# Fixed order of the first 512 tokens: k times u ahead of the copy of y, low parts one unit later, the third block's scans behind them

## The chip, the cores and the metric

The kernel runs on one core of a Trainium2 chip. The metric is device time in microseconds (us); the kernel before takes 1140.89 us, the median of three runs (1139.58 to 1141.2). TensorE is called PE, VectorE DVE, ScalarE ACT, GpSimd POOL and the queue that issues most transfers SP, as in the profile.

## What is computed

A linear attention over 768 tokens for 2 batches of 8 heads of width 48, then a two-layer SiLU network, then eight experts with ReLU, weighted by a table P that is normalised eight times over rows and columns:

```python
for t in range(S):                      # attention, per head
    cur = (u * k[t]) outer v[t]
    y[t] = r[t] @ (state + cur)
    state = w[t][:, None] * state + k[t] outer v[t]
x = silu(y @ w_in) @ w_out              # 1536 tokens, 384 -> 2048 -> 384
P = exp(x @ w_gate - max); 8 times: P /= P.sum(1); P /= P.sum(0); P *= N / E
out = sum_e P[:, e] * (relu(x @ w1[e]) @ w2[e])
```

## The kernel before

**Tiling.** The 1536 tokens are six blocks of 256; a unit is one block of one pair of heads, so a block has four units and the whole attention 24. Units 0 to 7 (the first two blocks, 512 tokens) are written out by `front()`, whose instructions keep the order in which they are written on each engine. Everything else (units 8 to 23, the split of the weights, the two networks) is ordered by a scheduler, which may put its instructions between those of `front()`.

**A unit** goes through five groups. `n_scan` (L180): on DVE a backward scan (`zf`, L191) and `kz` (L193); on ACT `uk`, k times u (L186). `n_q` (L196): PE multiplies `uk` (L202) and transposes `kz` (L207), ACT copies `kt` (L210), `tot` (L211) and, from unit 4 on, the state into a bank (L214). `n_x` (L220): on DVE a reciprocal (L223), a forward scan (L224) and `x` (L226). `n_s` (L228): PE's L233 needs `x`, its L238 needs `kt` and the state's copy. `n_m` (L241): DVE takes the banks to SBUF with L247, L248 and the scan over states L250. `n_y` (L253): PE makes y (L262, L264), ACT copies it to `ys` (L272), SP sends `ys` into the tile `x1` (L277). In `front()` step i emits unit i up to `n_s`, then `n_m` and `n_y` of unit i-1.

**High and low parts.** The matmuls of the networks work on a value as a high part rounded to fp32r and the low part that is left. `split_x1` (L426) makes them for a third of a block of y (128 of 384 rows): ACT casts `x1h` (L433), DVE subtracts to get `x1l` (L434). A third can be split once the copies of two neighbouring units have landed.

**Weights.** They come in 16 pieces of 768 KB, loaded from POOL (L91) into three buffers. A piece is brought from 64 to 32 bits on DVE (L135, L137, L138 in `narrow`), cast on ACT (`whi`, L113) and subtracted on DVE (`wlo`, L114). Piece 0 serves the first two steps of the first layer (L545 to L547, nine matmuls of 512 columns a step), piece 1 the first two of the second (L564 to L566), and so on in turn. The buffer of load 2 is the tile of `aux`, in which units 0 to 7 keep `tot`: it is free once L250 of unit 7 is done. ACT turns a bank of the first layer into `g` (L551) and `gh` (L552), DVE makes `gl` (L553).

**After the first two blocks**, `attn_a` (L307) takes the scans of units 8 to 11; the scheduler places them, and before the change it puts several among the instructions of unit 7. Each engine runs its queue in order.

Of the kernel before, what the change touches and what calls it, by code (L numbers as in the profile page):

```python
# [5 lines left out]
F32 = mybir.dt.float32  # L6
F32R = mybir.dt.float32r
I32 = mybir.dt.int32
ACTF = mybir.ActivationFunctionType
# [4 lines left out]
NP = H // 2  # L14
# [3 lines left out]
CH = 64  # L18
BLK = 256
# [4 lines left out]
OFF_K = OFF_R + BLK  # L24
OFF_V = OFF_K + BLK
ATW = OFF_V + 4 * D
LN = 64 + D
NU = 4 * NB
N4 = 2 * NP
# [4 lines left out]
C_U = C_ID + 128  # L34
# [21 lines left out]
class Pipeline:  # L56
# [123 lines left out]
    def n_scan(self, i):  # L180
        nc = self.nc
        p = i % NP
        at = self.at.pop(i)
        w, r, k = at[0:LN, 0:WPAD], *(at[0:LN, o:o + BLK].rearrange("p (c t) -> p c t", c=4) for o in (OFF_R, OFF_K))
        uk = self.q_p.tile([LN, 4, CH], F32, tag="rk", name="uk")
        nc.scalar.activation(uk, k, ACTF.Copy, scale=self.cst[0:LN, C_U + p:C_U + p + 1])  # L186
        zf, ef = (self.sc_p.tile([LN, 4, CH + 2], F32, tag=n, name=n) for n in ("zf", "ef"))
        kz = self.sc_p.tile([LN, 4, CH], F32, tag="kz", name="kz")
        zff, d1f = (t.rearrange("p c t -> p (c t)") for t in (zf, self.d1[i % 2]))
        n = WPAD  # L190
        nc.vector.tensor_tensor_scan(zff[:, n - 1::-1], w[:, n - 1::-1], d1f[:, n - 1::-1], 0.0,  # L191
                                     op0=ALU.mult, op1=ALU.add)
        nc.vector.tensor_mul(kz, k, zf[:, :, 2:CH + 2])  # L193
        self.st[i] = dict(zf=zf, ef=ef, kz=kz, r=r, w=w, uk=uk)

    def n_q(self, i):  # L196
        nc = self.nc
# [80 lines left out]

    def front(self):

        for i in range(N4 + 1):
            if i < N4:
                self.n_scan(i)
                self.n_q(i)
                self.n_x(i)
                self.warm(K['wm'])
                self.n_s(i)
                if i + 4 < NU:
                    self.attn_load(i + 4)
            if i == N4:  # L290
                self.split_pieces(1)
            if i > 0:
                self.n_m(i - 1)
                if i - 1 in K['gate']:
                    self.gates[self.n_dma] = self.attn_x(i - 1)[0:1, 1, 0, 0:1]
                    self.dma_pieces(self.n_dma + 1)
                self.n_y(i - 1)
                if i + 5 < NS:
                    self.attn_load_v(i + 5)
            if i > 2 and (i - 3) % NP > 0:  # L300
                self.split_x1((i - 3) // NP, (i - 3) % NP - 1)
        self.split_pieces(2)
        for j in (N4 - 2, N4 - 1):
            self.split_x1(j // NP, j % NP - 1)


    def attn_a(self, i):  # L307
        if i < NS:
            self.n_scan(i)
            self.n_x(i)  # L310
            return
        nc = self.nc
        p = i % NP
        at = self.at.pop(i)
        w = at[0:LN, 0:WPAD]
        r = at[0:LN, OFF_R:OFF_K].rearrange("p (c t) -> p c t", c=4)
        k = at[0:LN, OFF_K:OFF_V].rearrange("p (c t) -> p c t", c=4)
        vu = at[:, OFF_V:ATW].rearrange("p (j h e) -> p j h e", j=2, h=2)
        d1 = self.d1[i % 2]
        zf = self.sc_p.tile([LN, 4, CH + 2], F32, tag="zf", name="zf")  # L320
        ef = self.sc_p.tile([LN, 4, CH + 2], F32, tag="ef", name="ef")
        kz = self.sc_p.tile([LN, 4, CH], F32, tag="kz", name="kz")
        zff = zf.rearrange("p c t -> p (c t)")
        eff = ef.rearrange("p c t -> p (c t)")
        d1f = d1.rearrange("p c t -> p (c t)")
        n = WPAD
        nc.vector.tensor_tensor_scan(zff[:, n - 1::-1], w[:, n - 1::-1], d1f[:, n - 1::-1], 0.0,
                                     op0=ALU.mult, op1=ALU.add)
        nc.gpsimd.tensor_mul(kz, k, zf[:, :, 2:CH + 2])
        nc.vector.reciprocal(d1[:, :, 0:1], zf[:, :, 1:2])  # L330
        nc.vector.tensor_tensor_scan(eff, w, d1f, 0.0, op0=ALU.mult, op1=ALU.add)
        x = self.attn_x(i)
        if i < NS + 2:
            nc.gpsimd.memset(x[96:128, 1], 0.0)
        nc.vector.tensor_mul(x[0:64, 0], r[0:64], ef[0:64, :, 0:CH])
        nc.gpsimd.tensor_mul(x[64:LN, 1], r[64:LN], ef[64:LN, :, 0:CH])
        u = self.cst[0:LN, C_U + p:C_U + p + 1]
        rk = self.q_p.tile([LN, BLK], F32, tag="rk", name="rk")
        nc.vector.tensor_mul(rk, at[0:LN, OFF_R:OFF_K], at[0:LN, OFF_K:OFF_V])
        qh = self.q1_p.tile([LN, BLK], F32R, tag="qh", name="qh")  # L340
        ql = self.q1_p.tile([LN, BLK], F32R, tag="ql", name="ql")
        nc.scalar.activation(qh, rk, ACTF.Copy, scale=u)
        nc.vector.scalar_tensor_tensor(ql, rk, u, qh.bitcast(F32), op0=ALU.mult, op1=ALU.subtract)
        self.st[i] = dict(zf=zf, kz=kz, vu=vu, qh=qh, ql=ql)
# [79 lines left out]
        self.x1[blk] = self.x1_p.tile([128, 3, BLK], F32, tag="x1", name="x1")  # L424

    def split_x1(self, blk, c):  # L426
        nc = self.nc
        x1 = self.x1[blk]
        tb, h = divmod(blk, 2)
        if h == 0 and c == 0:  # L430
            self.xs[tb] = tuple(self.xs_p.tile([128, 3, 2 * BLK], F32R, tag="xs", name=n) for n in ("x1h", "x1l"))
        hi, lo = (t[:, :, h * BLK:(h + 1) * BLK] for t in self.xs[tb])
        nc.scalar.copy(hi[:, c, :], x1[:, c, :])  # L433
        nc.vector.tensor_sub(lo[:, c, :], x1[:, c, :], hi[:, c, :].bitcast(F32))  # L434

    def warm(self, n):

# [278 lines left out]
    def run(self):  # L716
        tc, nc = self.tc, self.nc
        with ExitStack() as ctx:
# [6 lines left out]
            self.wg = cst_p.tile([128, 3, E], F32, name="wg")  # L725
            self.ones = cst_p.tile([128, 128], F32, name="ones")
            self.P = cst_p.tile([128, 13, E + 1], F32, name="P")
            self.xs, self.x1, self.x2, self.x2s, self.h, self.acc, self.at, self.st = ({} for _ in range(8))
            gen = self.general
            if gen:  # L730
                nc.sync.dma_start(out=self.cst, in_=self.ins["cst"])
# [83 lines left out]
            for i in range(len(steps) + 2):  # L815
                if i < len(steps):
                    s = steps[i]
                    if s[0] == "m":
                        _, tb, o, n, f = s
# [19 lines left out]
                    else:  # L839
                        _, e, tb, f = s  # L840
# [3 lines left out]
                if i >= 2:  # L844
                    s = steps[i - 2]
                    if s[0] == "m":
                        _, tb, o, n, f = s
# [5 lines left out]
                    else:  # L853
                        _, e, tb, f = s
# [82 lines left out]
```

## Time and profile before

| What | Value |
|---|---|
| median of three runs | 1140.89 us |
| the profiled execution, its own time | 1140.3 us |
| span of the profiled execution | 1138.5 us |
| PE busy | 1111.7 us, 98% of the span |
| DVE busy | 477.4 us, 42% |
| ACT busy | 322.7 us, 28% |
| POOL busy | 152.9 us, 13% |

The shares are means over the program. In the first 80 us PE has gaps and its granted clock changes between its two levels, 1.2 and 2.4 GHz (0.5 and 1.0 in the rows below); later it does not. "Idle" in a row is the time just before an instruction, with what ended it; a start minus the start ahead of it is how long an engine was held by one instruction, a little less than its own duration.

### The profile page before, as it was taken

Reading aid. Unit: us, or ns where it says so; the run is one execution under the profiler, and the core shown is the slowest. Engines: PE = TensorE matmul, PEld = TensorE weight load, DVE = VectorE, ACT = ScalarE, POOL = GpSimd, SP = SyncE. Lnnn points to the kernel's source line nnn. Section 1 sums busy time; section 2 is a strip of 40 time slices with the busy share of each in tenths; the row PEclk is TensorE's granted clock in tenths of the full one; section 3 lists DMA queues with packets and bytes.
Section 4 is the critical chain, followed back from the end, with each engine's and each line's share of the span. In section 5 each row is a group of like instructions: output and inputs, shape, how many; then the busy total and the mean of one; then the engine's idle time right before and its main releaser. Section 6 shows DMA issues by size and latency. Waiting matters only on the chain.

```text
span 1138.5 us, 17570 instructions
## 1 busy us (share of the span) xinstructions
PE 1111.7 (98%) x7376; PEld 1003.5 (88%) x7376; DVE 477.4 (42%) x873; ACT 322.7 (28%) x615; POOL 152.9 (13%) x129
## 2 busy tenths in 40 slices
PE   7789999999999999999999999999999999999997
PEld 7668889999989999999999999889999989999996
DVE  6699767784443311222212422652364231222221
ACT  3344444444642242122113112321332231111110
POOL 1011111110640030013004001200220130000000
PEclk8779999999999999999999999999999999999999
DMA  6265412110330011002001300440252020000000
GB/s 197 82 230 175 137 49 70 57 36 9 112 112 1 1 59 53 1 21 91 1 1 56 111 1 4 163 139 29 83 167 84 1 84 1 1 1 1 28 29 31
DMA packets 26920, 71.26 MB, mean 63 GB/s; under 512 B 4128, under 2 KB 11280, under 8 KB 26832
## 3 DMA queue, kind: packets, MB, share of 16 engines
q1 hardware_dynamic: 24528, 57.46, 16.2%
q0 software_dynamic: 2304, 12.58, 3.5%
q8 instruction: 60, 0.98, 0.4%
q14 instruction: 28, 0.23, 0.1%
HBM read 65.31 MB, written 2.36 MB: 59 GB/s over the span
## 4 chain that ended last, share of the span: by engine, by line
PE 94%; DVE 2%; DMA 1%; ACT 1%; issue 0%; SPq 0%; DVEq 0%; ACTq 0%
PE bank L656 12%; PE bank L658 12%; PE bank L640 12%; PE bank L641 12%; PE bank L657 12%; PE bank L639 12%; PE bank L564 3%; PE bank L566 3%; PE bank L565 3%; PE bank L545 3%; PE bank L547 3%; PE bank L546 3%; PE bank L419 1%; PE bank L356 1%; DMA lv<-in_vn_dram 1%; PE bank L233 0%
## 5 line engine op out<-in xcount | busy, mean ns | idle before, releaser
L645 DVE SCALAR_TENSOR_TENSOR hl<-bank,hh 128x512 fp32r<-128x512 f32 x192 | 132.3, 690 | 434.4 <-ACT hh L644 434.0
L656 PE MATMUL bank<-whi,hh 128*128 128x384 f32 x768 | 258.9, 337 | 0.7 <-ACT hh L644 0.7
L657 PE MATMUL bank<-wlo,hh 128*128 128x384 f32 x768 | 258.2, 336 | 0.0
L658 PE MATMUL bank<-whi,hl 128*128 128x384 f32 x768 | 254.2, 337 | 0.0
L644 ACT ACTIVATE hh<-bank 128x512 fp32r<-128x512 f32 x192 | 114.6, 598 | 489.0 <-PE bank L641 478.4
L641 PE MATMUL bank<-x2h,wlo 128*128 128x512 f32 x576 | 227.9, 396 | 0.0
L640 PE MATMUL bank<-x2l,whi 128*128 128x512 f32 x576 | 227.5, 395 | 0.0
L639 PE MATMUL bank<-x2h,whi 128*128 128x512 f32 x576 | 224.5, 390 | 0.0
L114 POOL TENSOR_TENSOR wlo<-raw,whi 128x768 fp32r<-128x768 f32 x64 | 118.2, 1858 | 564.7 <-ACT whi L113 547.1
L656 PEld LDWEIGHTS bank<-whi,hh 128*128 128x128 f32 x768 | 144.3, 188 | 9.4 <-ACT hh L644 1.1
L657 PEld LDWEIGHTS bank<-wlo,hh 128*128 128x128 f32 x768 | 144.2, 188 | 8.0 <-issue 0.2
L658 PEld LDWEIGHTS bank<-whi,hl 128*128 128x128 f32 x768 | 143.9, 188 | 2.4
L641 PEld LDWEIGHTS bank<-x2h,wlo 128*128 128x128 f32 x576 | 108.0, 188 | 22.4
L639 PEld LDWEIGHTS bank<-x2h,whi 128*128 128x128 f32 x576 | 108.2, 188 | 17.2 <-issue 0.2
L640 PEld LDWEIGHTS bank<-x2l,whi 128*128 128x128 f32 x576 | 108.0, 188 | 17.2
L113 ACT CAST whi<-raw 128x768 fp32r<-128x768 f32 x64 | 53.3, 836 | 94.2 <-PE bank L640 40.9
L545 PE MATMUL bank<-x1h,whi 128*128 128x256 f32 (+1 forms) x240 | 74.2, 311 | 3.8 <-ACT g L551 2.8
L564 PE MATMUL bank<-gh,whi 128*128 128x256 f32 (+1 forms) x240 | 74.8, 317 | 0.0
L669 DVE SCALAR_TENSOR_TENSOR acc<-bank,P,acc 128x384 f32<-128x384 f32 x84 | 48.0, 611 | 63.7 <-PE bank L658 63.7
L546 PE MATMUL bank<-x1l,whi 128*128 128x256 f32 (+1 forms) x240 | 73.8, 308 | 0.0
L547 PE MATMUL bank<-x1h,wlo 128*128 128x256 f32 (+1 forms) x240 | 73.6, 308 | 0.0
L566 PE MATMUL bank<-gh,wlo 128*128 128x256 f32 (+1 forms) x240 | 73.2, 306 | 0.0
(156 smaller groups left out, 1131.8 us busy)
## 6 DMA issues: line engine op xcount, KB each, us to landing
raw<-in_moe_w_dram SPq DMA_DIRECT2D x64, 384.0 KB, 3.8
raw<-in_moe_w_in_dram POOLq DMA_DIRECT2D x8, 768.0 KB, 4.9
raw<-in_moe_w_out_dram POOLq DMA_DIRECT2D x8, 768.0 KB, 4.7
wh<-in_moe_w_in_dram SPq DMA_DIRECT2D x8, 768.0 KB, 4.3
wh<-in_moe_w_out_dram SPq DMA_DIRECT2D x8, 768.0 KB, 4.2
at<-in_att_dram SPq DMA_DIRECT2D x12, 484.0 KB, 3.5
at<-in_att_dram SPq DMA_DIRECT2D x11, 339.5 KB, 4.4
wt<-in_w_dram SPq DMA_DIRECT2D x3, 768.0 KB, 4.3
```

The lines of the kernel that those rows point to most:

```text
L114: (nc.vector if i < N64 else nc.gpsimd).tensor_sub(lo, raw, hi.bitcast(F32))
L545: nc.tensor.matmul(ps, lhsT=wh, rhs=xh[:, d, :], start=(d == 0), stop=False)
L546: nc.tensor.matmul(ps, lhsT=wh, rhs=xl[:, d, :], start=False, stop=False)
L564: nc.tensor.matmul(ps, lhsT=wdh, rhs=gh, start=first, stop=False)
L639: nc.tensor.matmul(ps, lhsT=wh, rhs=xh[:, d, :], start=(d == 0), stop=False)
L640: nc.tensor.matmul(ps, lhsT=wh, rhs=xl[:, d, :], start=False, stop=False)
L641: nc.tensor.matmul(ps, lhsT=wl, rhs=xh[:, d, :], start=False, stop=(d == 2))
L644: nc.scalar.activation(hh, ps, ACTF.Relu)
L645: nc.vector.scalar_tensor_tensor(hl, ps, 0.0, hh.bitcast(F32), op0=ALU.max, op1=ALU.subtract)
L656: nc.tensor.matmul(ps, lhsT=hh[:, sl], rhs=wh, start=st, stop=False)
L657: nc.tensor.matmul(ps, lhsT=hh[:, sl], rhs=wl, start=False, stop=False)
L658: nc.tensor.matmul(ps, lhsT=hl[:, sl], rhs=wh, start=False, stop=sp)
```

## The change

`uk` becomes a function of its own, `n_uk`. `front()` emits it for unit i+1 right behind `n_q(i)`, so ahead of the copy of y of unit i-1. `split_x1` is cut in two: the cast stays where it was, the subtraction is emitted in the next step, behind `n_x` and ahead of `n_m`. Behind unit 7 comes piece 0 of the weights, then the subtractions that are left, then piece 1. The DVE instructions of `n_scan` and `n_x` of units 8 to 11 are given an edge to the last of these subtractions: they are queued behind it on DVE. Their `uk` on ACT has no such edge.

```diff
 def n_scan(self, i):
-    uk = self.q_p.tile([LN, 4, CH], F32, tag="rk", name="uk")
-    nc.scalar.activation(uk, k, ACTF.Copy, scale=self.cst[0:LN, C_U + p:C_U + p + 1])
...
+def n_uk(self, i):
+    uk = self.uk[i] = self.q_p.tile([LN, 4, CH], F32, tag="rk", name="uk")
+    self.nc.scalar.activation(uk, self.at[i][0:LN, OFF_K:OFF_V]..., ACTF.Copy, scale=...)
...
 def front(self):
+    lag = []
+    self.n_uk(0)
     for i in range(N4 + 1):
         if i < N4:
             self.n_scan(i)
             self.n_q(i)
+            if i + 1 < N4:
+                self.n_uk(i + 1)
             self.n_x(i)
             self.warm(K['wm'])
             self.n_s(i)
...
-        if i == N4:
-            self.split_pieces(1)
+        while lag:
+            self.split_x1_low(*lag.pop())
         if i > 0:
             self.n_m(i - 1)
...
         if i > 2 and (i - 3) % NP > 0:
-            self.split_x1((i - 3) // NP, (i - 3) % NP - 1)
+            lag.append(((i - 3) // NP, (i - 3) % NP - 1))
+            self.split_x1_high(*lag[-1])
+    self.split_pieces(1)
+    self.split_x1_low(*lag.pop())
+    for j in (N4 - 2, N4 - 1):
+        self.split_x1_high(j // NP, j % NP - 1)
+        self.front_end = self.split_x1_low(j // NP, j % NP - 1)
     self.split_pieces(2)
-    for j in (N4 - 2, N4 - 1):
-        self.split_x1(j // NP, j % NP - 1)

 def attn_a(self, i):
     if i < NS:
-        self.n_scan(i)
-        self.n_x(i)
+        self.n_uk(i)
+        with self.tc.issue_after(self.front_end):
+            self.n_scan(i)
+            self.n_x(i)
         return
```

The new lines shift the numbers: in the rows of the changed kernel L197 is `uk` (L186 before), L214, L215 and L218 are `kt`, `tot` and the state (L210, L211, L214), L276 is `ys` (L272), L448 and L453 are the cast and the subtraction (L433, L434), L189, L191, L227, L228 and L230 are the DVE steps of `n_scan` and `n_x`, L251, L252 and L254 those of `n_m`.

ACT's queue from unit 4 to unit 5, before and after:

```order
L214 COPY bank_67<-ss_131 112x48
L272 COPY ys<-bank_65 112x256
L433 CAST x1h<-x_301 128x256
L186 ACTIVATE uk<-at,cst 112x256
L210 COPY kt<-bank_64 128x192
```

```order
L218 COPY bank_67<-ss_131 112x48
L197 ACTIVATE uk<-at,cst 112x256
L276 COPY ys<-bank_65 112x256
L448 CAST x1h<-x_303 128x256
L214 COPY kt<-bank_64 128x192
```

`uk` of unit 5 has moved from behind the copy of y and the cast to ahead of both.

DVE's queue at the same place, from the last step of unit 3 (L250, L254) to the first step of `n_m` of unit 4:

```order
L250 SCALAR_TENSOR_TENSOR ss_134<-bank_64,aux 112x288
L434 TENSOR_TENSOR x1l<-x_301,x1h 128x256
L191 SCALAR_TENSOR_TENSOR zf<-at,d_127 112x264
L193 TENSOR_TENSOR kz<-at,zf 112x256
L223 RECIPROCAL d_127<-zf 112x4
L224 SCALAR_TENSOR_TENSOR ef<-at,d_127 112x264
L226 TENSOR_TENSOR x_129<-at,ef 112x256
L247 TENSOR_TENSOR x_128<-bank_66,cst 128x256
```

```order
L254 SCALAR_TENSOR_TENSOR ss_134<-bank_64,aux 112x288
L189 SCALAR_TENSOR_TENSOR zf<-at,d_127 112x264
L191 TENSOR_TENSOR kz<-at,zf 112x256
L227 RECIPROCAL d_127<-zf 112x4
L228 SCALAR_TENSOR_TENSOR ef<-at,d_127 112x264
L230 TENSOR_TENSOR x_129<-at,ef 112x256
L453 TENSOR_TENSOR x1l<-x_303,x1h 128x256
L251 TENSOR_TENSOR x_128<-bank_66,cst 128x256
```

The subtraction has moved behind the five steps of unit 5.

DVE's queue behind unit 7's last step (L250, L254), where `x_601` and `x_603` are the second block of y; in the rows of after the second `cv<-raw` is piece 2 (the tile that held `aux`), the third piece 1:

```order
L250 SCALAR_TENSOR_TENSOR ss_134<-bank_64,aux 112x288
L247 TENSOR_TENSOR x_128<-bank_66,cst 128x256
L193 TENSOR_TENSOR kz<-at,zf 112x256
L248 COPY_PREDICATED x_128<-cst,bank_66 128x256
L250 SCALAR_TENSOR_TENSOR ss_131<-bank_67,xx 112x288
L191 SCALAR_TENSOR_TENSOR zf<-at,d_127 112x264
L223 RECIPROCAL d_127<-zf 112x4
L224 SCALAR_TENSOR_TENSOR ef<-at,d_127 112x264
L434 TENSOR_TENSOR x1l<-x_601,x1h 128x256
L135 TENSOR_SCALAR cv<-raw 128x768 x2
```

```order
L254 SCALAR_TENSOR_TENSOR ss_134<-bank_64,aux 112x288
L135 TENSOR_SCALAR cv<-raw 128x768
L137 SCALAR_TENSOR_TENSOR cv<-raw,cv 128x768
L138 SCALAR_TENSOR_TENSOR cv<-raw,cv 128x768
L114 TENSOR_TENSOR wlo<-cv,whi 128x768
L453 TENSOR_TENSOR x1l<-x_603,x1h 128x256
L135 TENSOR_SCALAR cv<-raw 128x768
L453 TENSOR_TENSOR x1l<-x_603,x1h 128x256
L137 SCALAR_TENSOR_TENSOR cv<-raw,cv 128x768
L453 TENSOR_TENSOR x1l<-x_603,x1h 128x256
L135 TENSOR_SCALAR cv<-raw 128x768
L189 SCALAR_TENSOR_TENSOR zf<-at,d_126 112x264
```

Before, all of piece 0 and the scans of units 8 to 10 stood ahead of the first of these rows; now they stand behind it, the scans behind the last subtraction.

## Rows read from the trace of the kernel before

**Rows 1.** Windows: stretch, length; busy PE, PEld, DVE, ACT, POOL; clock; DMA, GB/s.

```profile
84.20:1130.00 1045.80, 1045.14 (x6344) 946.66 (x6343) 411.06 (x738) 291.94 (x543) 146.03 (x101) 1.00 0.17 54
```

**Rows 2.** Windows of DVE alone, units 3 to piece 8: stretch, length, busy.

```profile
16.00:98.50 82.50, 65.39 (x123) 0.83 0.51 160
```

**Rows 3.** DVE's waits in 9 to 98.6 us: total, times, longest.

```profile
DVE x1l L434 <- ACT x1h L433: 10.6, 3, 5.5
DVE xx L247 <- PE bank L233: 2.2, 2, 1.5
DVE gl L553 <- ACT gh L552: 1.6, 2, 1.3
DVE cv L135 <- DMA raw<-in_moe_w_in_dram: 0.7, 1, 0.7
DVE wlo L114 <- ACT whi L113: 0.6, 2, 0.4
```

**Rows 4.** DVE: start, duration, instruction, idle before; subtraction in unit 4, unit 7's end.

```profile
31.28 0.43 DVE L434 TENSOR_TENSOR x1l<-x,x1h 128x256 fp32r<-128x256 f32 x1 [5.49 <-ACT x1h L433]
...
58.06 0.75 DVE L250 TENSOR_TENSOR_SCAN ss<-bank,aux 112x288 f32<-112x288 f32 x1
```

**Rows 5.** ACT in order of time: copy of y, cast.

```profile
30.57 0.37 ACT L272 COPY ys<-bank 112x256 f32<-112x256 f32 x1 [1.84 <-PE bank L264]
30.84 0.41 ACT L433 CAST x1h<-x 128x256 fp32r<-128x256 f32 x1
```

**Rows 6.** PE's waits in 0 to 80 us for `uk`: total, times, longest.

```profile
PE bank L202 <- ACT uk L186: 6.5, 7, 1.2
```

**Rows 7.** Windows, columns of rows 1: one unit; three stretches.

```profile
31.25:35.65 4.40, 3.49 (x66) 3.08 (x67) 4.15 (x9) 1.30 (x4) 0.00 (x0) 0.75 0.28 60
...
20.00:33.40 13.40, 9.95 (x260) 8.94 (x256) 6.99 (x16) 4.28 (x12) 0.71 (x2) 1.00 0.59 176
36.70:40.20 3.50, 1.88 (x51) 1.60 (x47) 1.95 (x5) 1.08 (x3) 0.00 (x0) 0.98 0.10 29
40.20:43.50 3.30, 3.30 (x58) 2.99 (x55) 2.17 (x5) 0.90 (x3) 0.00 (x0) 0.51 0.48 134
```

**Rows 8.** POOL in order of time: the issue of load 2.

```profile
59.38 0.53 POOL L91 DMA_DIRECT2D raw<-in_moe_w_in_dram  x1 [37.71 <-DVE x L247]
```

**Rows 9.** The page's line of loads of 768 KB: median us to landing last.

```profile
raw<-in_moe_w_in_dram POOLq DMA_DIRECT2D x8, 768.0 KB, 4.9
```

**Rows 10.** Copies of y, issued 54.2 to 56.5; 61.2 to 62.4.

```profile
DMA to landing us min/median/max: 1.8/1.9/1.9
...
DMA to landing us min/median/max: 5.4/5.6/5.8
```

**Rows 11.** DVE in order of time, at piece 8 of the weights.

```profile
97.63 0.95 DVE L138 SCALAR_TENSOR_TENSOR cv<-raw,cv 128x768 int32<-128x768 int32 x1
98.50 0.55 DVE L135 TENSOR_SCALAR cv<-raw 128x768 int32<-128x768 int32 x1
```

**Rows 12.** ACT in order of time, up to unit 10's state copy.

```profile
102.16 0.60 ACT L551 ACTIVATE g<-bank 128x512 f32<-128x512 f32 x1 [1.01 <-PE bank L547]
102.65 0.31 ACT L210 COPY kt<-bank 128x192 f32<-128x192 f32 x1
102.85 0.85 ACT L113 CAST whi<-cv 128x768 fp32r<-128x768 f32 x1
103.58 0.63 ACT L552 CAST gh<-g 128x512 fp32r<-128x512 f32 x1
104.10 0.26 ACT L214 COPY bank<-ss 112x48 f32<-112x48 f32 x1
```

**Rows 13.** PE in order of time, up to the states of unit 10.

```profile
108.12 0.39 PE L564 MATMUL bank<-gh,whi 128*128 128x512 f32 x1
108.34 0.39 PE L565 MATMUL bank<-gl,whi 128*128 128x512 f32 x1
108.66 0.56 PE L238 MATMUL bank<-lv,kt 64*48 64x48 f32 x16
```

More of the change, by code (lines that the diff above doesn't have):

```diff
@@ L193, in n_scan @@
         nc.vector.tensor_mul(kz, k, zf[:, :, 2:CH + 2])
-        self.st[i] = dict(zf=zf, ef=ef, kz=kz, r=r, w=w, uk=uk)
+        self.st[i] = dict(zf=zf, ef=ef, kz=kz, r=r, w=w, uk=self.uk.pop(i))
+    def n_uk(self, i):
+        p = i % NP
+        uk = self.uk[i] = self.q_p.tile([LN, 4, CH], F32, tag="rk", name="uk")
+        self.nc.scalar.activation(uk, self.at[i][0:LN, OFF_K:OFF_V].rearrange("p (c t) -> p c t", c=4), ACTF.Copy,
+                                  scale=self.cst[0:LN, C_U + p:C_U + p + 1])
     def n_q(self, i):
@@ L426, in split_x1, with split_x1_high @@
     def split_x1(self, blk, c):
-        nc = self.nc
-        x1 = self.x1[blk]
+        self.split_x1_high(blk, c)
+        self.split_x1_low(blk, c)
+    def split_x1_high(self, blk, c):
         tb, h = divmod(blk, 2)
@@ L431, in split_x1, with split_x1_low @@
             self.xs[tb] = tuple(self.xs_p.tile([128, 3, 2 * BLK], F32R, tag="xs", name=n) for n in ("x1h", "x1l"))
-        hi, lo = (t[:, :, h * BLK:(h + 1) * BLK] for t in self.xs[tb])
-        nc.scalar.copy(hi[:, c, :], x1[:, c, :])
-        nc.vector.tensor_sub(lo[:, c, :], x1[:, c, :], hi[:, c, :].bitcast(F32))
+        self.nc.scalar.copy(self.xs[tb][0][:, c, h * BLK:(h + 1) * BLK], self.x1[blk][:, c, :])
+    def split_x1_low(self, blk, c):
+        tb, h = divmod(blk, 2)
+        hi, lo = (t[:, c, h * BLK:(h + 1) * BLK] for t in self.xs[tb])
+        return self.nc.vector.tensor_sub(lo, self.x1[blk][:, c, :], hi.bitcast(F32)).ins
     def warm(self, n):
@@ L727, in run @@
             self.P = cst_p.tile([128, 13, E + 1], F32, name="P")
-            self.xs, self.x1, self.x2, self.x2s, self.h, self.acc, self.at, self.st = ({} for _ in range(8))
+            self.xs, self.x1, self.x2, self.x2s, self.h, self.acc, self.at, self.st, self.uk = ({} for _ in range(9))
             gen = self.general
```

## The prediction

> **What bounds the kernel now.** I read the windows first, then the waits, then single instructions in order of time. From 84.2 us to 1130 PE is busy for 1045.14 of 1045.80 us at clock 1.00 [rows 1]. Behind 84.2 us nothing but PE's own work sets the end, and the change alters none of it. So the time can only move with how much of its work PE has done by the end of the front, and the end moves one for one with that. The reader should look for the engine that kept PE waiting before. From unit 3 to piece 8 of the weights DVE is busy 65.39 of 82.50 us [rows 2], idle 82.50 - 65.39 = 17.1. Its largest wait is for the cast `x1h`: 10.6 us in three waits, the longest 5.5 [rows 3]. There DVE is free at 31.28 - 5.49 = 25.8 and stands until the cast that follows `ys` is made [rows 4, 5], though five steps of the next unit's scans are ready behind it in its queue. PE meanwhile waits for `uk` seven times, 6.5 us together [rows 6], since `uk` stands on ACT behind the same copy and cast. The two waits feed each other: `ys` needs y, y comes late on a PE that waited for `uk`, and the subtraction waits for all of it. The narrowing of the weights comes behind this on DVE, so what DVE loses in the front arrives at the weights.
>
> **What the change removes.** `uk` ahead of `ys` needs only `at`, and a buffer that L202 of two units earlier has left; PE's waits of 6.5 / 7 = 0.93 each go. The subtraction one unit behind finds its cast made while DVE did the five steps of the next unit. Nearly the same DVE instructions stand ahead of L138 of piece 8 in both orders: the order of after has, net, three fewer steps of 128x256 of units 8 and 9 there. At 0.4 each, as L434 takes [rows 4], that is 1.1 us. So the sum is a ledger of DVE's idle time up to that step, which before hands on at 98.50 [rows 11].
>
> **What stays or comes anew**, term by term.
>
> *Subtractions.* The first still waits. Its cast follows `ys` of unit 3, which ended y at about 30.5 before; less three of the `uk` waits (2.7) this is 27.8, and with copy and cast (0.27 and 0.31 as queue steps [rows 5]) 28.5. DVE, free at 25.8 before, gains 1.9 on its waits for L233 (below), then does five steps, 2.5 of a unit's 4.15 [rows 7]: 26.4. Wait 2.1. The following units start from a PE that no longer waits, and I take nothing for them. The last needs unit 7's copies. Copies landed in 1.8 to 1.9 us while the queue was empty and in 5.4 to 5.8 around the time of the loads [rows 10]. In the order of after, loads 2 and 3 are under way there too. Counting from the end T of unit 7's L250: y and its copy 1.3, the last of the issues about 1.4 later, 5.6 to land, the cast 0.3, together 8.6. DVE gets to the last subtraction at T + 7.2. Wait 1.4; with 1.9 to land, none. Together 3.5, where 10.6 stood.
>
> *Banks of L233.* They waited 2.2 because PE came late with `uk`; I leave 0.6.
>
> *Loads.* Load 2 goes into `aux`, free with L250 of unit 7. That ended at 58.06 + 0.75 = 58.8, and POOL issued at 59.38 [rows 4, 8]: 0.6 later, and 4.9 to land [rows 9], so T + 5.4 or a little more. DVE has piece 0 (0.47 and three steps of 0.87), a wait for `whi` and one subtraction ahead of piece 2: T + 4.3. Wait 1.1. Before, seven steps of units 8 to 10 and all of piece 0 covered this. Load 6 waits in the same way for piece 3's buffer, 0.5 + 4.9 = 5.4 against 3.9 of DVE work queued: 1.5. Together 2.6, where 0.7 stood [rows 3].
>
> *Low parts of the weights.* `wlo` of piece 0 now follows its narrowing at once with the cast (0.73 as a queue step [rows 12]) between: 1.1, where 0.6 stood [rows 3].
>
> *Others.* Before: 17.1 - 10.6 - 2.2 - 0.7 - 0.6 = 3.0, of which 1.6 for `gh` [rows 3]. I take 1.6, bounds 1.0 and 3.0.
>
> *Unit 7 alone.* Scans of units 8 to 10 filled the gaps between its dependent steps; without them I estimate 0.5.
>
> Sum 3.5 + 0.6 + 2.6 + 1.1 + 1.6 + 0.5 = 9.9. So 17.1 - 9.9 = 7.2 less idle, with the 1.1 some 8.2, and piece 8's step hands on at 98.5 - 8.2 = 90.3.
>
> **From DVE to PE.** In the order of after the last wait of PE that I find stands in front of L242, the states of unit 10 (L238 before). It needs ACT's copy of the state, which is queued behind `whi` of piece 8 (0.73), `g` (0.49), `gh` (0.52), `kt` (0.20) and takes 0.2 [rows 12]; with 0.26 for the handings over, 2.4. PE begins it at 90.3 + 2.4 = 92.7, before at 108.66 [rows 13]: 16.0 earlier. But less of PE's work stands ahead of it: by the order 117 wide matmuls instead of 137, 20 at 108.34 - 108.12 = 0.22 to 0.23 each [rows 13], 4.55, and one unit's y less, 0.14. PE gains 16.0 - 4.7 = **11.3 us**. That this is more than DVE's 8.2 comes from slack: before, the split pieces lay some microseconds ahead of PE, and after they do not. Behind this, DVE needs less for a piece than PE, and PE stays supplied.
>
> The profiled execution took 1140.3, its span 1138.5; both move alike, to 1129.0. The median lies 0.6 higher: 1140.9 - 11.3 = **1129.6**.
>
> **Other moves.** SP: the load of unit 11's `at` stands behind unit 7's copies; its scans are now late on DVE, so nothing. POOL: loads 2, 3, 5, 4, 6 in this order, and unit 12's `kz` with a memset ahead of load 12, which waits about as long for the buffer of piece 9; nothing. ACT: the casts stand a `uk` later, 0.4, covered by the five steps of the next unit except at the first cast, where it is in the 2.1. The clock: for 13.4 us at 9.95 busy the granted clock stayed at 1.00 [rows 7], and after a thinner stretch, 1.88 of 3.5, it fell to 0.51 in the next [rows 7]. DVE's 4.15 us a unit now paces PE, whose 9.95 / 13.4 share rises, so I leave the front at full clock. The Trainium skill ("DMA: Bandwidth & Descriptors", section "Issuing engines are not separate DMA queues") says that transfers started by different engines run on the same 16 DMA engines and interleave. By it the copies of unit 7, issued from SP, share with POOL's loads of 768 KB; rows 10 agree. It speaks against moving subtractions close behind those copies: without it the 1.4 would be 0 and the time 1128.2.
>
> **Rivals.**
> *Faster still.* Copies land in 1.9 (1.4 less) and load 6 finds its buffer early enough (1.5 less, less 0.6 that PE can't take up): 13.6 in all, 1127.3. For it: the loads start earlier against the copies than before. Against it: 5.4 to 5.8 once measured [rows 10]. Chance 0.15.
> *The clock falls.* DVE alone serves units 5 to 7, and PE stands between units. If it goes to its lower level, as in 40.2 to 43.5 (0.51) after a stretch with PE busy for about half [rows 7], PE's part of a unit is as long as DVE's and y, `ys` and cast come later: some 2 us, 1131.5. The Trainium skill ("TensorE: Matmul & The Clock Gate", section "HAM oscillation — how this bites in real kernels") tells the same of bursts with waits between; the two last windows of rows 7 agree. Chance 0.12.
> *It doesn't do what it says.* The subtraction waits in each unit as at the first, since y of unit i comes after the states of unit i+1 on PE: three times 2.1 instead of once, 4.2 more, with some 0.3 for what hangs behind: 1134. For it: ACT's `kt` and state copy stand behind the cast. Against it: five steps of cover. Chance 0.11.
> *Slower.* All scans of units 8 to 11, and all pieces from 1 on, hang in DVE's queue behind the last subtraction, and that hangs on unit 7's copies. Each us by which these land later costs one. It decides from 5.6 + 11.3 = 17 us of landing; at 20 the kernel would take 1144. The longest seen is 5.8 [rows 10]; but three loads of 768 KB in front of the copies would make 3 x 4.9 = 15 if they were served one after another. Chance 0.05.
> *Eaten later.* A wait behind piece 8 takes the gain up to 2 us, as PE's work ahead of unit 10 has become less: 1139 to 1141. Chance 0.05.
>
> **How the numbers follow.** Forecast 0.52 at 1129.6; the rest as above. The range goes from 1126.0 (the faster rival with the other waits at 1.0 and unit 7 at no cost, another 1.1) to 1135.0 (the third rival with the others near 3.0), which leaves out the last two cases and the ends of the rest, 0.2. A measurement of this kernel tells 0.2%, 2.3 us, from no change: faster 0.90, same 0.05, slower 0.05.
>
> **What would show it.** In the profile of after: no waits of L206 for `uk` in units 1 to 7; waits of L453 for L448 of about 2 at the first, near 0 at the next two and about 1.4 at the last; waits of L135 for loads 2 and 6 near 1.1 and 1.5; L138 of piece 8 ending its step near 90.3; L242 of unit 10 near 92.7 and PE without gaps behind; PE's clock at 1.00 from 20 to 60 us. Wrong would be: waits of 2 or more at each L453 (third rival), clock rows near 0.5 between 43 and 70 us (second), PE gaps behind 93 us (the slack was larger or a later piece late), or copies that land in over 6 us.

## The result, and the profile after

The changed kernel takes 1128.87 us, the median of four runs (1127.9 to 1130.4), beside 1140.24 (1138.73 to 1141.2) for the kernel before on the same chip: 11.4 us less, ratio 0.9903, 95% interval 0.9886 to 0.992. The forecast was 1129.6. The profiled execution took 1127.9 with a span of 1126.0, the one before 1140.3 and 1138.5; the difference of the spans, 12.5 us, is taken apart below. One execution of e2 below ran in a slow state (1806.2 us at a mean granted clock of 0.554) and is left out of every number.

As before, PE alone sets the end behind the front. Windows of the whole core (stretch, length; busy time and count of PE, PEld, DVE, ACT, POOL; PE clock, DMA share, GB/s):

```profile
91.00:1117.00 1026.00, 1025.28 (x6214) 929.66 (x6211) 396.72 (x720) 283.00 (x528) 141.94 (x96) 1.00 0.16 52
```

PE is idle for 0.7 of 1026 us, which answers [rows 1]; its last wait of the front now ends at 91 us. DVE alone, from unit 3 to the moment at which piece 8's narrowing hands on, and then the two rows of DVE at that place (start, duration, instruction):

```profile
16.00:88.17 72.17, 63.70 (x119) 0.93 0.56 173
```

```profile
87.30 0.95 DVE L138 SCALAR_TENSOR_TENSOR cv<-raw,cv 128x768 int32<-128x768 int32 x1
88.17 0.68 DVE L572 TENSOR_TENSOR gl<-g,gh 128x512 fp32r<-128x512 f32 x1
```

Idle time is 72.17 - 63.70 = 8.5 us where it was 17.1 [rows 2], and 1.7 us less work stands in the stretch; together 10.3, so piece 8 hands on at 88.17 and not at 98.50 [rows 11]. The same from the start of the program, before and after (stretch, length, DVE busy and count):

```profile
0.00:98.50 98.50, 76.97 (x151) 0.83 0.56 170
```

```profile
0.00:88.17 88.17, 75.90 (x148) 0.92 0.61 181
```

So only 1.1 us of the 1.7 is work that no longer stands ahead (three steps); the other 0.6 is idle time that DVE had lost ahead of 16 us and no longer loses. What DVE still waits for in 9 to 95 us (total, times, longest):

```profile
DVE cv L135 <- DMA raw<-in_moe_w_in_dram: 2.5, 1, 2.5
DVE x1l L453 <- DMA lv<-in_vn_dram: 2.5, 1, 2.5
DVE x1l L453 <- ACT x1h L448: 1.0, 1, 1.0
DVE wlo L114 <- ACT whi L113: 0.9, 1, 0.9
DVE gl L572 <- ACT gh L571: 0.5, 1, 0.5
DVE ss L254 <- PE bank L242: 0.4, 1, 0.4
```

The three waits of 10.6 us for the cast in [rows 3] have become two, 2.5 and 1.0; the waits for L233's banks are gone; a wait of 2.5 for load 2 is new. The second row names `lv`, but L453 reads only y and its cast, so what it waited for stands on ACT, under the third question. PE's waits up to 110 us, the three that answer to [rows 6] and to the forecast of its last wait:

```profile
PE bank L564 <- ACT x1h L448: 2.3, 1, 2.3
...
PE bank L242 <- ACT bank L218: 2.2, 2, 1.5
...
PE bank L206 <- ACT uk L197: 0.7, 1, 0.7
```

The 6.5 us in seven waits for `uk` are one of 0.7. PE's last wait is this one (idle before in brackets), where [rows 13] had its L238:

```profile
90.82 0.56 PE L242 MATMUL bank<-lv,kt 64*48 64x48 f32 x16 [1.45 <-ACT bank L218]
```

### The profile page after: what moved, and what is told of

Read it like the earlier page. It is cut to its first block, busy times and chain, and to the rows that moved or that the text cites. A ratio compares the mean times of both kernels' runs of the same rounds, so it can differ in the third digit from the quotient of the medians.

```text
span 1126.0 us, 17562 instructions
## 1 busy us (share of the span) xinstructions
PE 1103.7 (98%) x7376; PEld 995.3 (88%) x7376; DVE 477.6 (42%) x873; ACT 322.5 (29%) x615; POOL 151.2 (13%) x129
## 4 chain that ended last, share of the span: by engine, by line
PE 89%; DMA 4%; issue 2%; DVE 2%; POOL 1%; ACT 1%; SPq 0%; DVEq 0%; POOLq 0%; ACTq 0%
PE bank L675 12%; PE bank L677 11%; PE bank L676 11%; PE bank L659 11%; PE bank L660 11%; PE bank L658 11%; PE bank L583 3%; PE bank L585 3%; PE bank L584 3%; PE bank L564 3%; PE bank L566 3%; PE bank L565 3%; DMA raw<-in_moe_w_in_dram 1%; DMA wh<-in_moe_w_in_dram 1%; DMA lv<-in_vn_dram 1%
## 5 line engine op out<-in xcount | busy, mean ns | idle before, releaser
L584 PE MATMUL bank<-gl,whi 128*128 128x256 f32 (+1 forms) x240 | 73.2, 306 | 0.0
```

## The experiments

The changed kernel was timed in two sets of runs, with medians of 1128.9 and 1129.7; the kernel before stood in four, with medians of 1140.2 to 1143.3, and its executions scattered from 1135.7 to 1148.3. So e1 to e4 are set against before in their own set, whose median was 1143.3, e6 to e8 against the changed kernel in theirs (e5), and differences under some 1.5 us between sets are left open.

**First question: which part of the change carries the gain?** Theory: DVE's list sets the front, and PE's waits for `uk` and DVE's waits for the cast feed each other, so neither part alone gives all. Rivals: one part carries everything.

*e1*, `uk` alone:

```diff
         for i in range(N4 + 1):
                 self.n_q(i)
+                if i + 1 < N4:
+                    self.n_uk(i + 1)
                 self.n_x(i)
```

> The kernel before with one part of the change alone: uk of the next unit ahead of the copy of y on ACT; the subtractions stay behind their cast. Theory (DVE sets the front, and the waits for uk and for the cast feed each other): PE's 6.5 us of waits for uk go, DVE's 2.2 for L233 go, and the waits for the cast shrink from 10.6 to 6 or 7, since y comes earlier; 5 to 6 us faster, 1134 to 1135. Rival 1 (the uk move carries everything, the order on DVE is of no account): 1129 to 1130. Rival 2 (the cast still holds DVE, PE only waits elsewhere): within 2 us of before, 1139 or 1140.

Measured 1136.5 (1135.3 to 1137.1), ratio to before 0.9914 (0.9892 to 0.9937). Two rows of DVE's and PE's waits:

```profile
DVE x1l L442 <- ACT x1h L441: 10.5, 3, 4.0
```

```profile
PE bank L211 <- DVE kz L191: 4.8, 3, 1.9
```

The waits for `uk` went, but the cast still held DVE for 10.5 us, not the 6 or 7 of the theory: y came earlier, and so did DVE. PE now waits for DVE's `kz`, 4.8 us. In this set 6.9 us were gained, about half of what the whole change brings; rival 1 falls.

*e2*, the subtraction one unit behind, alone:

```diff
+            while lag:
+                self.split_x1_low(*lag.pop())
             if i > 0:
                 self.n_m(i - 1)
...
-                self.split_x1((i - 3) // NP, (i - 3) % NP - 1)
+                lag.append(((i - 3) // NP, (i - 3) % NP - 1))
+                self.split_x1_high(*lag[-1])
```

> The kernel before with the subtractions one unit behind and nothing else; uk still stands behind the copy of y and the cast. Theory: five steps of the next unit, 2.5 us, cover each of three waits for the cast (10.6 in all), about 3 remain at the first, and PE still waits 0.9 for uk in each unit, which becomes a wait of DVE for L233; 4 to 5 us faster, 1135 to 1136. Rival (the subtraction is what held everything): 1130 to 1132. If PE's uk waits are what paces the front: within 2 us of before.

Measured 1142.1, the median of nine, ratio 0.9984 (0.9945 to 1.0022): as a median nothing that can be told from the kernel before. But the nine fall into two groups. Four took 1133.6 to 1137.5 at a mean granted clock of 0.982 to 0.984, around the 1135 to 1136 expected, and five took 1142.1 to 1146.0 at 0.968 to 0.976. The only trace kept is of one of the short ones (1135.4, 4.9 less than the profiled execution of before); its waits:

```profile
DVE x1l L444 <- ACT x1h L439: 4.9, 2, 3.1
DVE xx L247 <- PE bank L233: 2.1, 2, 1.4
```

```profile
PE bank L202 <- ACT uk L186: 6.8, 7, 1.3
```

The waits for the cast fell from 10.6 to 4.9, while those for L233's banks (2.2 before) and for `uk` (6.5) stayed as they were: they did not take up what the cast gave, as the expectation had it. So what the subtraction brings alone is open.

*e3*, both together, everything behind unit 7 as before:

> Both of the first two parts, uk ahead and subtractions one unit behind, but piece 0, the scans of units 8 to 10 and the last subtractions ordered as before. Theory: nearly all of the idle time of DVE that the change removes is removed here, 8 to 10 us faster, 1130 to 1132; what is left to the third part is a wait or two behind unit 7. Rival (the order behind unit 7 is worth as much as the rest): 1134 or more.

Measured 1131.0 (1130.3 to 1133.1), ratio 0.9868 (0.9843 to 0.9893). That is 5.5 us less than e1, with no overlap of the two: once `uk` is ahead, the subtraction is worth that much, and the rival of 1134 or more falls. Whether the two parts together bring more than each by itself can't be told from the times: e1 and e2 add up to 1.0 per cent, e3 has 1.3, and the intervals are 0.2 to 0.4 wide to either side.

*e4*, the changed kernel with the scans of units 8 to 11 free again:

```diff
-            with self.tc.issue_after(self.front_end):
-                self.n_scan(i)
-                self.n_x(i)
+            self.n_scan(i)
+            self.n_x(i)
```

> The changed kernel without the edge that holds the scans of units 8 to 11 behind the last subtraction: on DVE they stand among unit 7's steps again, piece 0 and the subtractions as in the changed kernel. Theory: scans move, DVE's total does not; they fill some of the 2.5 us in which DVE waited for load 2 and lengthen unit 7 by their own 5 or 6 us; the time stays within 1.5 us of the changed kernel, 1128 to 1130.5. Rival (holding the scans back is where the gain is): 1132 or more.

Measured 1132.9 (1132.2 to 1134.9): 3 to 4 us behind the changed kernel and no better than e3. Here the rival was right. DVE's waits in 9 to 98 us, the largest five:

```profile
DVE gl L571 <- ACT gh L570: 2.5, 4, 1.5
DVE xx L251 <- PE bank L237: 2.3, 2, 1.9
DVE x1l L452 <- DMA x<-ys: 2.0, 1, 2.0
DVE x1l L452 <- ACT x1h L447: 1.7, 1, 1.7
DVE x L251 <- PE bank L237: 1.2, 2, 0.9
```

With four smaller ones (1.0, 0.7, 0.6, 0.2) these make 12.2 us, where the changed kernel's list above makes 7.8: 4.4 more. The two profiled executions lie 7.0 apart (1134.9, the longest of e4's four, and 1127.9, the shortest of the changed kernel's), so DVE's waits are not all of it. The total of DVE's work doesn't change, but with the scans between, the last step of unit 7 starts at 47.22 and not at 38.58, and everything that hangs on unit 7 (its copies, the last cast, the first layer, `g`) comes later. PE shows it too, here with DVE's L252 of unit 6:

```profile
43.68 0.44 DVE L252 COPY_PREDICATED xx<-cst,bank 128x256 f32<-128x256 int32 x1
```

```profile
44.22 0.91 PE L206 MATMUL bank<-at,uk 64*64 64x64 f32 x12 [3.88 <-issue]
```

The profile names nothing that PE waited for in these 3.88 us, but it goes on 0.1 us after DVE's late step on unit 6's bank has ended, and e3's trace has the same 3.88 at the same place. From 44.2 to 50 us PE's clock is then 0.50. e3's listed waits of DVE add up to 7.9 us, no more than the changed kernel's. So how much of the 3 to 4 us is DVE's idle time and how much PE's stand with the low clock behind it was not separated. The prediction had credited nothing to the edge itself.

**Second question: is it DVE that sets the end?** Theory: yes, one for one. Rivals: PE with its clock, which fell to its lower level behind unit 7, or another engine.

*e5*, the changed kernel as reference:

> The changed kernel itself, as the reference on this chip for the three runs beside it. Theory: 1128 to 1130 again, and a scatter of 3 us or less; if the kernel before scatters by 10 us on the same chip, the scatter belongs to its order and not to the chip.

Measured 1129.7 (1128.9 to 1130.5); before, in the same runs, 1136.7 to 1147.8. The scatter belongs to the order.

*e6*, six more subtractions where DVE is packed:

```diff
-                self.split_x1_low(*lag.pop())
+                for _ in range(4 if i in (6, 7) else 1):
+                    self.split_x1_low(*lag[-1])
+                lag.pop()
```

> The changed kernel with the subtractions of units 6 and 7's steps made four times instead of once: six more subtractions of 0.34 us, 2.0 us of DVE work in the front where DVE is packed, and nothing else on PE's or ACT's path. Theory (DVE's list sets the end): 1.5 to 2.0 us slower than the changed kernel. Rival (PE and its clock set it, DVE has slack): within 0.5 us of it.

Measured 1132.9 (1131.5 to 1134.3), 3.2 more than e5. The dose was larger than meant; DVE in order of time:

```profile
38.03 1.79 DVE L455 TENSOR_TENSOR x1l<-x,x1h 128x256 fp32r<-128x256 f32 x4
39.74 0.41 DVE L251 TENSOR_TENSOR xx<-bank,cst 128x256 f32<-128x256 f32 x1
...
41.97 0.75 DVE L254 TENSOR_TENSOR_SCAN ss<-bank,aux 112x288 f32<-112x288 f32 x1
```

Four on the same tile hold DVE for 39.74 - 38.03 = 1.71, where one holds it for 0.33 in e5's profile, so the six are 2.8 and not 2.0; unit 7's last step starts at 41.97, in e5's profile at 39.17, 2.8 later. 2.8 in and 3.2 out: DVE paces the front, and the rival that gives it slack falls. The way to the end was not the same, though: PE's last wait stands at 71.1 us in e6's profile and at 91.0 in e5's, so that the two numbers are near each other is not traced step by step.

*e7*, nine small matmuls on PE behind unit 7's y:

```diff
+        self.warm2(4)
         self.split_pieces(1)
...
             nc.tensor.matmul(ps, lhsT=wl, rhs=xh[:, d, :], start=False, stop=(d == 2))
+            if i == 0 and d == 0:
+                self.warm2(5)
```

> The changed kernel with nine small matmuls on PE behind unit 7's y, where PE stood about 2 us and then 2.3 us waiting and its clock fell to 0.50 from 46 to 52 us. They fill most of that wait and hold the clock up. Theory (DVE sets the end): PE does its first wide matmuls earlier and waits later; within 1 us of the changed kernel. Rival (the low clock, 6 us at half speed there and 3 us more later, is time lost): 3 to 4 us faster, 1125.

Measured 1127.8 (1125.8 to 1128.7), 1.9 less than e5: between the two expectations. Windows of the changed kernel behind unit 7, of e7 at the answering place, and then of e5 and e7 behind it (columns as above):

```profile
42.60:47.00 4.40, 1.47 (x4) 0.59 (x4) 1.83 (x3) 0.82 (x3) 0.00 (x0) 0.81 0.91 327
47.00:53.00 6.00, 5.85 (x14) 4.29 (x14) 4.94 (x9) 1.59 (x4) 0.36 (x1) 0.57 0.02 7
```

```profile
50.00:59.00 9.00, 4.99 (x32) 3.43 (x33) 7.63 (x15) 4.86 (x9) 1.05 (x2) 0.98 0.26 79
```

```profile
59.00:70.00 11.00, 9.41 (x105) 6.93 (x105) 11.00 (x22) 4.68 (x9) 0.92 (x2) 1.00 0.26 77
```

```profile
59.00:70.00 11.00, 11.00 (x80) 8.58 (x78) 11.00 (x22) 4.91 (x10) 0.00 (x0) 0.86 0.43 145
```

In the changed kernel PE stood for 2.9 of 4.4 us and then worked at a clock of 0.57; in e7 the clock is 0.98 at that place, but 0.86 from 59 to 70 us, where e5 has 1.00. The low clock was in part only moved. The profiled executions of e7 and e5 lie 0.3 us apart (1128.7 and 1128.9), and the scheduler placed some instructions behind 60 us in another order. So the 1.9 between the medians is not the clock's price; what the low clock costs there stays open.

*e8*, piece 1 ahead of the last two subtractions, piece 2 behind them:

```diff
         self.split_pieces(1)
         self.split_x1_low(*lag.pop())
+        self.split_pieces(2)
         for j in (N4 - 2, N4 - 1):
             ...
-        self.split_pieces(2)
+        self.split_pieces(3)
```

> The changed kernel with piece 1 of the weights ahead of the last two subtractions and piece 2 behind them: DVE then narrows piece 1, which is long there, in the 2.5 us in which it waited for load 2 and the 1.0 us in which it waited for unit 7's copies. Theory: 2 to 3.5 us of idle time of DVE are filled; 2 to 3 us faster than the changed kernel, 1126. Rival (behind unit 7 another engine is late next, PE after its wait for the last cast or ACT): within 1 us of it.

Measured 1126.4 (1125.8 to 1128.6), 3.2 less than e5, as the theory has it, and the lowest median of all the kernels. The profiled execution is the longest of the four (1128.6), so its rows show less than that gain. DVE's rows between piece 0 and the last subtraction, and PE's window behind:

```profile
45.15 0.42 DVE L454 TENSOR_TENSOR x1l<-x,x1h 128x256 fp32r<-128x256 f32 x1
45.48 0.55 DVE L135 TENSOR_SCALAR cv<-raw 128x768 int32<-128x768 int32 x1
46.07 0.96 DVE L137 SCALAR_TENSOR_TENSOR cv<-raw,cv 128x768 int32<-128x768 int32 x1
47.06 0.96 DVE L138 SCALAR_TENSOR_TENSOR cv<-raw,cv 128x768 int32<-128x768 int32 x1
48.91 0.96 DVE L114 TENSOR_TENSOR wlo<-cv,whi 128x768 fp32r<-128x768 f32 x1 [0.90 <-ACT whi L113]
```

```profile
70.00:115.00 45.00, 45.00 (x393) 35.25 (x389) 44.18 (x74) 20.52 (x37) 11.08 (x15) 1.00 0.65 211
```

All of piece 1 lies where the changed kernel waited for load 2. PE's wait of 1.45 ahead of unit 10's L242 is gone: PE is gapless from 70 us on, 21 us earlier than in the changed kernel. The last subtraction still waits 0.90 for its cast, and DVE's listed waits up to 98 us add up to 7.5, in e5's profile to 7.9: what shrank is less the sum than the part that PE still hung on.

**Third question: why did the first subtraction wait 2.5 us?** The prediction put it down to PE's y. The trace of the changed kernel shows a second cause, ACT in order of time:

```profile
26.85 0.37 ACT L276 COPY ys<-bank 112x256 f32<-112x256 f32 x1 [2.34 <-DMA x<-ys]
27.12 0.41 ACT L448 CAST x1h<-x 128x256 fp32r<-128x256 f32 x1
```

`ys` of unit 3 stood until copies of unit 1 had left its buffer. These copies landed late; first the kernel before, then the changed one, copies issued in 14 to 32 us:

```profile
DMA to landing us min/median/max: 1.9/2.4/4.6
```

```profile
DMA to landing us min/median/max: 2.5/4.1/6.8
```

*e9*, the load of piece 1, which started at 18.8 us among them, gated by unit 4 instead of unit 2:

```diff
-K = {'tk': (4, 0, 2, 4, 6), 'wr': (4, 0), 'wm': 1, 'gate': (0, 2)}
+K = {'tk': (4, 0, 2, 4, 6), 'wr': (4, 0), 'wm': 1, 'gate': (0, 4)}
```

> The changed kernel with the load of piece 1 gated by unit 4 instead of unit 2, so that it starts some 10 us later, behind the copies of units 1 to 3; every queue of PE, DVE and ACT is the same. In the changed kernel ACT's copy of y of unit 3 waited 2.3 us for copies of unit 1 to leave their buffer, which took up to 6.8 us to land. Theory (the load of 768 KB delays the copies, and these the first subtraction): that wait falls under 1 us, DVE's first wait for a cast from 2.5 to under 1, and the time by 1 to 2 us against the changed kernel, 1128; PE, busy for 16 of 17 us there, can't take up all of it. Rival (the first subtraction waits for PE's y, as the prediction had it): wait and time as before it, within 0.5 us.

Measured 1128.9 (1128.4 to 1129.8). In the same stretch the copies landed sooner, and the next cause stood behind; landing, then ACT, then DVE:

```profile
DMA to landing us min/median/max: 1.8/2.9/5.7
```

```profile
27.35 0.37 ACT L276 COPY ys<-bank 112x256 f32<-112x256 f32 x1 [1.40 <-PE bank L268]
```

```profile
28.06 0.42 DVE L453 TENSOR_TENSOR x1l<-x,x1h 128x256 fp32r<-128x256 f32 x1 [1.64 <-DMA lv<-in_vn_dram]
```

The wait for the buffer is gone, ACT now waits for PE's y, and 1.64 of DVE's 2.5 us stay. The other traces say how much of this is the load's doing. With the load moved (e9, e10, e12) the copies landed in medians of 2.9 to 3.4 us, with the load where it was (changed kernel, e3 to e8, e11) in 3.6 to 5.2: it does delay them. But the wait for the buffer, which none of the three has, is also missing in e3, e4, e6 and e11. Where it is missing, the first subtraction waits 1.6 to 1.7 us for y (e3, e6, e9, e10, e12; in e4 2.0, for a copy that landed late). So y was a cause, as predicted, and the buffer adds to it in some executions only, 0.9 in the changed kernel's trace. The 1 to 2 us expected did not come.

*e10*, e8 with e9's gate:

> Piece 1 ahead of the last two subtractions (e8) and the load of piece 1 gated by unit 4 (e9) together. Theory: the gains add, since they are idle stretches of DVE at different places: 4 us faster than the changed kernel, 1125 to 1126. Rival (from 1126.4 on PE's own work sets the front): as e8, 1126 to 1127; slower if piece 1 now comes too late for its narrowing.

Measured 1129.1 (1128.0 to 1131.4). The gains do not add; e9 by itself had brought none.

*e11*, e8 with the first subtraction a further unit behind:

```diff
-            while lag:
+            while lag and i != N4 - 3:
```

> e8 with the first subtraction a further unit behind, next to the second, while the load of piece 1 stays where it was: DVE no longer meets the late copies. Theory: DVE's first wait of 2.5 us goes, and 1 to 2 us against e8, 1125; ACT's wait for the buffer stays. Rival (ACT's late copy of y holds PE or the next casts, so the wait only moves to the following unit): within 0.5 us of e8.

Measured 1127.4 (1124.9 to 1128.4). The rival was right: the first two subtractions, now next to each other, wait together one unit later.

```profile
32.41 0.76 DVE L454 TENSOR_TENSOR x1l<-x,x1h 128x256 fp32r<-128x256 f32 x2 [1.73 <-ACT x1h L449]
```

The wait was 1.86 in e8's profile, and the time isn't better than e8's.

*e12*, e10 with the nine matmuls behind unit 7's y in one block:

```diff
+        self.warm2(9)
         self.split_pieces(1)
```

> e10 with nine small matmuls on PE behind unit 7's y, which keep its clock up while it waits for the last cast. Theory: DVE's idle stretches are filled, so that PE's own rate behind unit 7 counts now, and a higher clock at 46 to 52 us brings what it didn't in e7 alone: 1 to 2 us against e10, 1124. Rival (DVE still sets the end): within 0.5 us of e10.

Measured 1128.6 (1128.3 to 1128.9), within 0.5 us of e10, as the rival has it. In the profiles of e10 to e12 PE is gapless from 70 us on, as in e8, and has its last long wait ahead of that for the cast of unit 7's copies (1.6, 1.6 and 2.5 us). So in those three nothing that DVE loses behind 70 us reaches the end. What sets the time at which PE gets there was not taken apart: e10 to e12 ran on another chip than e8, and they lie between 1127.4 and 1129.1 with scatters of 0.6 to 3.5 us.

## Why the prediction was right, point by point

**What bounds the kernel.** That the end moves with DVE's list is shown by e6 (2.8 in, 3.2 out). That nothing else moves it is not shown: e7, with no change to DVE's list, came out 1.9 lower.

**The two removed waits.** That taking both away brings more than `uk` alone is shown by e3 against e1 (5.5 us). That they feed each other is not shown: with `uk`'s waits gone, e1's waits for the cast stayed at 10.5, and e2's times leave open what the subtraction does by itself. The rival that the change doesn't do what it says is out: the two middle subtractions found their cast made, and units 4 to 6 followed each other on DVE at 4.14 us, the 4.15 of [rows 7], as their last steps show:

```profile
28.86 0.75 DVE L254 TENSOR_TENSOR_SCAN ss<-bank,aux 112x288 f32<-112x288 f32 x1
...
33.00 0.75 DVE L254 TENSOR_TENSOR_SCAN ss<-bank,aux 112x288 f32<-112x288 f32 x1
...
37.14 0.75 DVE L254 TENSOR_TENSOR_SCAN ss<-bank,aux 112x288 f32<-112x288 f32 x1
```

**The ledger.** Predicted 9.9 of remaining idle, measured 8.5:
- subtractions 3.5; measured 2.5 + 1.0 = 3.5. That the size came out right is luck: y of unit 3 was done at about 25.8, not 27.8, DVE was free at 25.1, not 26.4, and 0.9 of the first wait came from a buffer that ACT waited for.
- L233's banks 0.6; measured none.
- loads 2.6; measured 2.5, but all of it at load 2, which was counted at 1.1. POOL issued it at 39.62 and DVE could start at 46.47, 6.85 later and not the 4.9 of [rows 9], with load 3 and unit 7's copies under way beside it. Load 6, counted at 1.5, held nothing.
- low parts 1.1; measured 0.9.
- others and unit 7 alone, 1.6 + 0.5; measured 0.5 for `gl` and about 1.1 in gaps too small for the list.

DVE's work ahead of the handing on was 76.97 - 75.90 = 1.1 less, as counted. So piece 8 handed on 10.3 earlier, not 8.2: 1.4 from the ledger, in which the terms for the banks, the low parts and the gaps were put too high, and 0.6 from idle time ahead of 16 us, which the ledger left out; the two errors in the loads cancelled.

**From DVE to PE.** 2.4 was worked out; 90.82 - 88.17 = 2.65 was measured, with `whi`, `g`, `gh`, `kt` and the state's copy in that order on ACT. L242 came 108.66 - 90.82 = 17.8 earlier; less the 4.7 counted for PE's work that stands behind it now, 13.1. The spans differ by 12.5: from this instruction to the end it is 1035.2 us, where it was 1029.8, 5.3 longer and not 4.7. The wide matmuls ahead are 117 and were 137, as counted; which of PE's other work the 0.6 is was not traced. The medians differ by 11.4, since the profiled execution is the shortest of its four. So the forecast of 11.3 is nearer to the medians than its steps deserve: by the profile alone it was 1.2 low.

**The clock.** The forecast of full speed from 20 to 60 us was wrong. The mean of this stretch is 0.87; row 47.00:53.00 above has 0.57, and 56 to 59.3 us is at 0.54:

```profile
56.00:59.30 3.30, 3.30 (x10) 2.59 (x9) 3.30 (x7) 1.73 (x5) 0.00 (x0) 0.54 0.86 286
```

The rival of the falling clock had the right mechanism at another place, behind unit 7 instead of between units 5 to 7. What it cost is open (e7); part of it is hidden, since PE waited again behind it for DVE's and ACT's steps (0.67, 0.90, 0.70 and 1.45).

A rival that the prediction did not name is that the whole gain comes from the clock: PE does the same 7376 matmuls in both kernels, and of the 12.5 us between the spans 8.0 lie in its busy time (1111.7 and 1103.7) and 4.5 in its idle time. The stretch from 20 to 60 us in before, e3 and the changed kernel:

```profile
20.00:60.00 40.00, 29.59 (x610) 26.56 (x608) 27.86 (x62) 12.53 (x35) 1.33 (x4) 0.80 0.40 115
```

```profile
20.00:60.00 40.00, 32.82 (x669) 28.70 (x664) 34.75 (x71) 15.30 (x43) 2.31 (x6) 0.79 0.57 174
```

```profile
20.00:60.00 40.00, 32.17 (x553) 26.89 (x553) 32.35 (x65) 18.20 (x45) 2.11 (x4) 0.87 0.60 179
```

e3's profiled execution is 9.0 us shorter than that of before at the same clock here, 0.79 and 0.80: for the first two parts the clock is not the cause. The last 3.4 us, from e3 to the changed kernel, come with a clock of 0.87 and with no less idle time of DVE (7.9 and 7.8), so there it may be a part of the cause.

**Other moves.** "Nothing" was right for SP and POOL. The edge that holds the scans back was not costed as a part of its own; e4, in another set than the changed kernel, gives it 3 to 4 us.

**Slower.** The last subtraction did hang on unit 7's copies. The last cast began at 48.94, after ACT had waited for their landing; copies issued in 36 to 50 us landed in 5.6 (median) and at most 6.2, far from 17.

## What to carry to other kernels

Where two engines wait on steps of one loop, take both waits away: `uk` alone brought 0.9% (e1), both 1.3% (e3), and the subtraction alone nothing that stands clear of its scatter (e2). Make a ledger of the idle time of the engine that paces, before and after, and look at each new wait for work that is already there and stands behind it in the queue; piece 1, behind a wait for load 2, was worth another 3.2 us by the medians. Work that is free to move isn't neutral: put between the steps of the last unit, it delays all that hangs on that unit.

## What was not expected of the hardware

In the packed front the transfers landed later: the copies of y issued in 14 to 32 us went from a median of 2.4 to 4.1 us, the load of 768 KB among them from 4.8 to 7.5, and load 2 took 6.7. The Trainium skill ("DMA: Bandwidth & Descriptors", section "Issuing engines are not separate DMA queues") has transfers of different engines interleave on the same 16 DMA engines. The traces of e9, e10 and e12 agree: with the load from POOL moved back by some 10 us, the copies from SP landed in 2.9 to 3.4.

The kernels with `uk` behind the copy of y (before and e2) scatter over 12 us from one execution to the next, the twelve with `uk` ahead over 4 or less, in four to eight executions each. In e2 and in the runs of before beside e9 to e12 the time follows the mean granted clock: in these runs of before four took 1138.7 to 1141.2 at 0.982 to 0.986, and three 1146.5 to 1147.7 at 0.968 to 0.970. Beside e1 to e8 long executions of before, up to 1148.0, also come at 0.985 to 0.988, so the cause is open.
